# A fused linear-attention and highway kernel: a new order of all engines, eight half steps that read x from PSUM, six joint turns of k and q, and weights loaded by column halves

## The chip, the core and the metric

The kernel runs on one core of a Trainium2 chip. The metric is the device time of one execution in microseconds (us). The engines are TensorE (PE, with its weight loads as PEld), VectorE (DVE), ScalarE (ACT), GpSimd (POOL) and SyncE (SP); in this kernel SP only issues the DMA transfers.

## The reference

Two parts are computed one after the other: a linear attention with a decay per head, and a highway layer on its output.

```python
# batch 4, heads 8, sequence 768, head_dim 64; blocks of 64 positions
intra = einsum('bhic,bhjc->bhij', qb, kb) * Dmask[None]        # decay lam ** (i - j), causal
intra = einsum('bhij,bhjd->bhid', intra, vb)
inter = einsum('bhid,bhde->bhie', qb * lam_pow[None], kv_state)
out[:, :, sl] = intra + inter
kv_state = lam_block * kv_state + einsum('bhsd,bhse->bhde', kb_dec, vb)
...
x = out.transpose(0, 2, 1, 3).reshape(3072, 512)
H = maximum(x @ w_h, 0.0)
T = 1.0 / (1.0 + exp(-(x @ w_t + b_t)))
return T * H + (1.0 - T) * x                                    # float32
```

## The kernel before

**The work.** The 3072 rows are cut into twelve steps, n = 0 to 11, of 256 positions each: three steps for each batch element. A step has two half steps, b = 0 and 1, of 128 positions. For a step the kernel loads q, k and v (six transfers of 256 KB, two halves of each), casts q and k to bf16 (`CQ`, `CK`), multiplies v by powers of the decay (`CV`), and turns q and k on PE so that the head dimension lies on the partitions: `RQF` and `RKF` are eight 128x128 transposes each, into one PSUM bank each, and `EQ`/`EK` copy the result to SBUF in two halves. In step 10 `RK` and `RQ` do the same with 64-row transposes into two banks that k and q share (sixteen transposes each, L260), and `FK`/`FQ` copy them out; this is called a joint turn. Scores (`S`, L273) and the running state (`U`, L278; `KE` copies the state to SBUF) follow; `SA`/`SB` are pieces in which scores and state updates alternate. `M` masks the scores (DVE, L315), `I` (L334) and `A` (L343) give the attention output in two PSUM banks, and `D` (DVE, L349) scales it into `xT`, which is x turned.

**A half step of the highway layer.** x is turned back on PE (`TXB`, four 128x128 transposes, L362; or `TX`, sixteen 64-row transposes of a whole step, L371) and copied from PSUM to SBUF as `xs` (`XC`, ACT or DVE). `BP` puts the bias into a bank; `F.n.b.1` adds x @ w_t to it and `F.n.b.0` makes x @ w_h in another bank (four matmuls of 512 columns each, L386). Then `H` makes y = max(h, 0) - x (DVE, L399), `G` the sigmoid g (ACT, L404), `X` y = g * y (POOL or DVE, L408) and `Y` ob = y + x (POOL or DVE, L412). `ST` stores a step's 512 KB. The last half step, 11.1, is split: `P` = g * x (L415), `R` = x - P (L418), and for three column pieces `HX` = max(h, 0) * g (L422) and `YL` (L426) add the two.

**What sets the order.** No scheduler is at work. `PLAN` is a list of tokens such as `F.7.0.1.2`, `CK.9.2@ACT` or `TXB.6.1=6`, gone through from the left; each token issues its instructions on its engine, so that the order on one engine is the order of its tokens in the list. `@` names the engine, the digits behind `=` name the PSUM banks. There are seven such banks, 0 to 6, beside the bank of the running state. A token that takes a bank waits until the last reader of its former content is done. `Lq`, `Lk`, `Lv`, `W` and `ST` are transfers, all on SP's queue, at most eight of them under way at a time (L193). `W.w.g` loads half of a weight matrix (w = 1 is w_t, 0 is w_h), `WC.w.g.i` casts a quarter of one. `Z` are idle matmuls on PE at the start. The buffers in SBUF are rings: g has three, y and ob six, xs and xT three.

Of the kernel before, what the change touches and what calls it, by code (L numbers as in the profile page):

```python
# [21 lines left out]
WC.1.1.1@DVE Z.3=0 KE.1.0@ACT D.0.0@DVE Lv.2.1 WC.1.0.1@ACT WC.1.0.0@POOL M.1.0.1 U.1.1 TXB.0.0=0 BP.0.0.2@ACT=3
M.1.1.1 I.1=64 KE.1.1@ACT D.0.1@DVE F.0.0.1.2 Lk.3.1 WC.0.1.1@POOL WC.0.1.0@ACT M.1.0.0 BP.0.1.2@ACT=1 TXB.0.1=5 A.1.1
G.0.0.2 A.1.0 Lk.3.0 WC.0.0.1@DVE F.0.1.1.2 WC.0.0.0@ACT D.1.1@DVE XC.0.2.1@ACT Lq.3.1 F.0.1.0.2=2 D.1.0@DVE
XC.0.2.0@ACT Lq.3.0 G.0.1.2@S BP.1.1.2@DVE=4 TXB.1.1=5 F.0.0.0.2=0 H.0.1.2 Lk.5.1 CQ.2.2@ACT XC.1.2.1@DVE F.1.1.1.2
X.0.1.2@POOL H.0.0.2 Lv.3.1 CK.2.2@ACT BP.1.0.2@DVE=6 RQF.2=5 Lv.3.0 G.1.1.2@S Y.0.1.2@POOL TXB.1.0=1 X.0.0.2@DVE
RKF.2=2 XC.1.2.0@ACT F.1.1.0.2=0 EQ.2.1@DVE Lq.5.1 EK.2.0@ACT EK.2.1@DVE CV.2.2@POOL EQ.2.0@ACT S.2.1=14 Lk.4.1
H.1.1.2 F.1.0.1.2 M.2.0.1 Lk.5.0 CK.3.2@ACT S.2.0=25 M.2.1.1 X.1.1.2@POOL U.2.0 Lq.4.1 F.1.0.0.2=1 M.2.1.0 KE.2.0@ACT
Lq.4.0 CQ.3.2@ACT Y.0.0.2@POOL M.2.0.0 I.2=45 H.1.0.2 RKF.3=3 Lq.5.0 G.1.0.2@S A.2.1 Y.1.1.2@POOL EK.3.0@DVE
EK.3.1@ACT A.2.0 RQF.3=2 Lk.4.0 D.2.1@DVE X.1.0.2@POOL EQ.3.0@ACT D.2.0@DVE TXB.2.1=3 Lv.4.1 F.2.1.0.2=0  # L30
BP.2.1.2@ACT=1 EQ.3.1@DVE Lv.4.0 CV.3.2@POOL BP.2.0.2@DVE=6 XC.2.2.1@ACT TXB.2.0=2 F.2.1.1.2 H.2.1.2 XC.2.2.0@ACT
Lv.5.1 S.3.1=32 G.2.1.2@S S.3.0=54 Lq.6.1 Y.1.0.2@POOL M.3.0.1 U.3.0 CK.5.2@ACT F.2.0.0.2=0 Lq.6.0 M.3.1.0
X.2.1.2@POOL KE.3.0@ACT M.3.0.0 F.2.0.1.2 Lk.6.1 H.2.0.2 Lv.5.0 RKF.5=3 CQ.4.2@POOL G.2.0.2@S M.3.1.1 I.3=45 U.3.1
Lk.6.0 CK.4.2@ACT EK.5.1@DVE A.3.0 CQ.5.2@POOL A.3.1 EK.5.0@DVE RQF.4=2 D.3.0@DVE Lk.7.0 KE.3.1@ACT RKF.4=3
Y.2.1.2@POOL D.3.1@DVE BP.3.0.2@ACT=1 RQF.5=0 Lv.6.1 EQ.4.0@DVE EK.4.1@ACT TXB.3.0=6 TXB.3.1=4 EQ.5.0@DVE CV.4.2@POOL
F.3.1.0.2=5 EQ.5.1@ACT XC.3.2.0@DVE EK.4.0@DVE XC.3.2.1@ACT EQ.4.1@DVE S.5.0=60 H.3.1.2 F.3.0.1.2 CQ.6.2@ACT
X.2.0.2@POOL M.5.1.0 Lv.8.1 SA.4=3 M.5.0.0 Lv.6.0 S.4.1=42 BP.3.1.2@ACT=5 F.3.0.0.2=0 M.4.1.0 Y.2.0.2@POOL Lq.7.0
KE.4.0@ACT M.4.1.1 G.3.0.2@S F.3.1.1.2 Lk.8.1 CV.5.2@POOL H.3.0.2 CK.6.2@ACT SB.4=6 M.4.0.1 S.5.1=32 I.4=10 M.4.0.0
KE.4.1@ACT RKF.6=4 G.3.1.2@S M.5.0.1 X.3.0.2@POOL Lv.9.1 U.5.0 EK.6.0@ACT A.4.0 M.5.1.1 A.4.1 Lq.7.1 KE.5.0@ACT
RQF.6=6 X.3.1.2@POOL D.4.0@DVE EK.6.1@ACT Lq.8.0 I.5=32 EQ.6.1@DVE BP.4.0.2@ACT=5 TXB.4.0=1 Lq.9.1 D.4.1@DVE A.5.1  # L40
CV.6.2@POOL A.5.0 Lv.7.0 XC.4.2.0@DVE F.4.0.0.2=4 D.5.0@DVE Lk.7.1 D.5.1@DVE TXB.4.1=1 BP.5.0.2@ACT=0 Lk.8.0 TXB.5.0=3
F.4.0.1.2 Y.3.1.2@POOL H.4.0.2 XC.4.2.1@ACT Lv.7.1 XC.5.2.0@ACT BP.5.1.2@DVE=2 TXB.5.1=1 Lk.10.0 F.5.0.0.2=4 G.4.0.2@S
Y.3.0.2@POOL EQ.6.0@DVE Lv.8.0 XC.5.2.1@ACT BP.4.1.2@DVE=5 SA.6=3 Lq.9.0 X.4.0.2@POOL S.6.1=61 H.5.0.2 KE.6.0@ACT
F.5.0.1.2 Lk.9.1 M.6.1.0 CQ.7.2@POOL F.4.1.1.2 M.6.0.1 Lk.9.0 G.5.0.2 M.6.1.1 F.5.1.0.2=3 Y.4.0.2@POOL Lq.8.1
CK.7.2@ACT X.5.0.2@DVE F.4.1.0.2=6 H.5.1.2 G.4.1.2 CK.8.2@POOL Lk.11.0 RKF.7=1 Lk.10.1 H.4.1.2 SB.6=4 CV.7.2@POOL
EK.7.1@ACT RQF.7=0 EK.7.0@DVE KE.6.1@ACT M.6.0.0 I.6=13 RKF.8=6 EQ.7.1@ACT X.4.1.2@DVE A.6.0 EQ.7.0@ACT CV.8.2@POOL
# [450 lines left out]
```

## Time and profile before

| | |
|---|---|
| device time, median of 3 runs | 105.09 us (105.09 to 105.13) |
| device time of the profiled execution | 104.68 us |
| its span, first to last instruction | 102.9 us |
| PE busy | 92.4 us, 90% of the span |
| DVE busy | 87.2 us, 85% |
| POOL busy | 78.9 us, 77% |
| ACT busy | 76.8 us, 75% |
| transfers of SP's queue | 27.27 MB, 87.4% of 16 DMA engines |

The profiled execution's device time is 1.78 us above its span. Busy times are of single instructions laid over each other; matmuls are pipelined, so that a busy PE need not be at its peak. A line with "idle before" tells how long the engine stood still before an instruction and what ended it. "Issue" is time in which nothing that the profile shows was waited for. Line numbers are those of the kernel before; behind L232 the changed kernel's lines are higher (the masks stand at L316, H at L417, X at L426, Y at L429).

### The profile page before, as it was taken

Reading aid. Unit: us, or ns where it says so; the run is one execution under the profiler, and the core shown is the slowest. Engines: PE = TensorE matmul, PEld = TensorE weight load, DVE = VectorE, ACT = ScalarE, POOL = GpSimd, SP = SyncE. Lnnn points to the kernel's source line nnn. Section 1 sums busy time; section 2 is a strip of 40 time slices with the busy share of each in tenths; the row PEclk is TensorE's granted clock in tenths of the full one; section 3 lists DMA queues with packets and bytes.
Section 4 is the critical chain, followed back from the end, with each engine's and each line's share of the span. In section 5 each row is a group of like instructions: output and inputs, shape, how many; then the busy total and the mean of one; then the engine's idle time right before and its main releaser. Section 6 shows DMA issues by size and latency. Waiting matters only on the chain.

```text
span 102.9 us, 4082 instructions
## 1 busy us (share of the span) xinstructions
PE 92.4 (90%) x1706; PEld 57.4 (56%) x1725; DVE 87.2 (85%) x164; ACT 76.8 (75%) x132; POOL 78.9 (77%) x78
## 2 busy tenths in 40 slices
PE   5997998899898999999999989999999899999900
PEld 1443565556376668458654865846745746555400
DVE  4237989599898799999999799797997999999960
ACT  3599974999968878989587679995996675584600
POOL 6704452406999999999989995999999969689540
PEclk9999999999999999999999999999999999999997
DMA  1999999999999999999999999999991361415243
GB/s 19 272 312 317 292 369 387 354 307 287 297 322 331 329 283 293 292 294 310 331 310 300 314 310 317 323 335 395 403 380 70 128 255 37 156 48 202 111 164 138
DMA packets 33479, 27.52 MB, mean 267 GB/s; under 512 B 1460, under 2 KB 26420, under 8 KB 33461
## 3 DMA queue, kind: packets, MB, share of 16 engines
q1 hardware_dynamic: 33456, 27.27, 87.4%
q8 instruction: 13, 0.21, 0.9%
q14 instruction: 6, 0.04, 0.1%
q10 hardware_dynamic: 4, 0.00, 0.0%
HBM read 20.97 MB, written 6.29 MB: 265 GB/s over the span
## 4 chain that ended last, share of the span: by engine, by line
PE 61%; ACT 10%; SPq 9%; DMA 8%; issue 4%; DVE 3%; POOLq 1%; POOL 1%; ACTq 0%
PE bt L386 17%; PE bh L386 16%; SPq L194 9%; DMA w_f<-in_moe_w_t_dram 8%; PE bs L273 5%; PE bo L343 5%; PE bo L334 4%; PE kv L278 3%; PE bktr L244 3%; PE bx L362 3%; PE bqtr L244 3%; ACT kT L113 2%; ACT w_b L113 2%; ACT g L404 2%; ACT xs L113 1%
## 5 line engine op out<-in xcount | busy, mean ns | idle before, releaser
L315 DVE TENSOR_TENSOR m<-bs,tri 128x512 bf16<-128x512 f32 x48 | 30.8, 682 | 0.9 <-PE bs L273 0.9
L386 PEld LDWEIGHTS <-xT 128*128 128x128 bf16 x200 | 17.1, 98 | 16.9 <-issue 0.4
L408 POOL TENSOR_TENSOR y<-g,y 128x512 bf16<-128x512 f32 x17 | 19.7, 1161 | 8.1 <-DVE y L399 6.0
L412 POOL TENSOR_TENSOR ob<-y,xs 128x512 f32<-128x512 bf16 x21 | 24.1, 1159 | 0.6 <-DVE y L408 0.3
L386 PE MATMUL bh<-w_b,xT 128*128 128x512 bf16 (+2 forms) x94 | 23.8, 362 | 0.6 <-issue 0.2
L232 POOL TENSOR_TENSOR vs<-vf,pow_v 128x1024 bf16<-128x1024 f32 (+1 forms) x12 | 21.9, 1835 | 3.0 <-DMA vf<-in_v_dram 2.9
L386 PE MATMUL bt<-w_b,xT 128*128 128x512 bf16 x89 | 23.3, 380 | 0.9 <-issue 0.8
L349 DVE TENSOR_TENSOR xT<-bo,pow_o 128x512 bf16<-128x512 f32 x24 | 15.9, 683 | 0.4 <-PE bo L343 0.3
L399 DVE SCALAR_TENSOR_TENSOR y<-bh,xs 128x512 bf16<-128x512 f32 x23 | 15.6, 685 | 0.6 <-PE bh L386 0.2
L404 ACT ACTIVATE g<-bt 128x512 f32<-128x512 f32 x18 | 10.8, 598 | 4.3 <-PE bt L386 4.2
L113 ACT ACTIVATE ss<-kv 128x512 bf16<-128x512 f32 x19 | 11.3, 593 | 3.5 <-PE kv L278 3.4
L273 PE MATMUL bs<-qT,kT 64*64 64x128 bf16 x384 | 11.7, 220 | 0.5 <-ACT qT L113 0.3
L113 ACT ACTIVATE bt<-b_bc 128x512 f32<-128x512 f32 x18 | 10.7, 601 | 1.6 <-DVE xT L349 1.0
L273 PEld LDWEIGHTS <-kT 64*64 64x64 bf16 x384 | 8.1, 106 | 3.2 <-DVE kT L115 1.1
L113 ACT ACTIVATE kb<-kf 128x1024 bf16<-128x1024 f32 x9 | 9.5, 1059 | 0.2 <-DMA kf<-in_k_dram 0.2
L278 PE MATMUL kv<-vs,kb 64*64 64x64 bf16 x320 | 8.9, 195 | 0.7 <-issue 0.7
L278 PEld LDWEIGHTS <-kb 64*64 64x64 bf16 x320 | 6.9, 109 | 3.9 <-issue 2.9
L113 ACT ACTIVATE xs<-bx 128x512 bf16<-128x512 bf16 x13 | 7.5, 593 | 1.2 <-PE bx L362 0.9
L343 PE MATMUL bo<-m,vs 64*64 64x128 bf16 x384 | 8.2, 218 | 0.2 <-DVE m L315 0.2
L113 ACT ACTIVATE kT<-bktr 128x512 bf16<-128x512 bf16 x10 | 6.0, 597 | 2.8 <-DVE kT L115 1.5
L115 POOL CAST qb<-qf 128x1024 bf16<-128x1024 f32 (+1 forms) x6 | 5.8, 972 | 2.8 <-DMA qf<-in_q_dram 2.8
L115 DVE COPY kT<-bktr 128x512 bf16<-128x512 bf16 x12 | 5.0, 421 | 3.4 <-PE bktr L244 2.1
(72 smaller groups left out, 135.2 us busy)
## 6 DMA issues: line engine op xcount, KB each, us to landing
qf<-in_q_dram SPq DMA_DIRECT2D x24, 256.0 KB, 5.1
kf<-in_k_dram SPq DMA_DIRECT2D x24, 256.0 KB, 5.4
vf<-in_v_dram SPq DMA_DIRECT2D x24, 256.0 KB, 5.4
out_dram<-ob SPq DMA_DIRECT2D x11, 512.0 KB, 4.9
w_f<-in_moe_w_t_dram SPq DMA_DIRECT2D x2, 512.0 KB, 6.8
w_f<-in_moe_w_h_dram SPq DMA_DIRECT2D x2, 512.0 KB, 9.5
out_dram<-ob SPq DMA_DIRECT2D x1, 256.0 KB, 2.0
out_dram<-ob SPq DMA_DIRECT2D x2, 64.0 KB, 1.6
```

Source lines behind the costliest of these rows:

```text
L113: A.activation(dst, src, AF.Copy)
L232: ENG[eng].tensor_tensor(buf("vs", n)[:, hs], in0=buf("vf", n)[:, hs].rearrange("p h (j d) -> p h j d", j=J), in1=pow_v[:, n % NST, hs, :, ...
L273: T.matmul(get("s", n, e, hp // 2)[half(b), hp % 2, j, :], lhsT=buf("kT", n)[half(e), hp, j, half(b)], rhs=q_cols(n, half(e), hp, b), star ...
L278: T.matmul(kv[half(e), hp, half(e)], lhsT=buf("kb", n)[half(b), j, 2 * hp + e, :], rhs=buf("vs", n)[half(b), 2 * hp + e, j, :], start=firs ...
L315: V.tensor_tensor(buf("m", n, e, u), in0=get("s", n, e, u), in1=tri[:, None].to_broadcast([128, 2, J, C]), op=ALU.mult)
L343: T.matmul(get("o", n, b)[half(e), hp, :], lhsT=buf("vs", n)[half(b), 2 * hp + e, j, :], rhs=buf("m", n, e, hp // 2)[half(b), hp % 2, j, : ...
L349: V.tensor_tensor(cut(buf("xT", n)[:, :, b * C:(b + 1) * C]), in0=get("o", n, b).rearrange("e k (j p) -> e k p j", j=Q), in1=cut(pow_o[:, ...
L386: T.matmul(t, lhsT=buf("xT", n)[:, j, b * C:(b + 1) * C], rhs=w_b[w][:, j, z], start=(j == 0 and not w), stop=(j == KC - 1), skip_group_ch ...
L399: V.scalar_tensor_tensor(buf("y", n, b)[:, z], in0=get("h", n, b, p), scalar=0.0, in1=buf("xs", n)[:, b, z], op0=ALU.max, op1=ALU.subtract)
L404: A.activation(buf("g", n, b)[:, cols(p)] if to == "S" else t, t, AF.Sigmoid)
L408: ENG[eng].tensor_tensor(y, in0=buf("g", n, b)[:, cols(p)] if eng == "POOL" else get("t", n, b, p), in1=y, op=ALU.mult)
L412: ENG[eng].tensor_tensor(buf("ob", n)[:, b, z], in0=buf("y", n, b)[:, z], in1=buf("xs", n)[:, b, z], op=ALU.add)
```

## The change

All of `PLAN` is written anew. Beside the order of the tokens, four things in it differ.

- **Eight half steps (0.0, 0.1, 1.0, 4.0, 4.1, 10.0, 10.1, 11.0) read x from PSUM.** `XC`, `H`, `X` and `Y` are gone there. In their place `RP` makes r = (g - 1) * x with x read from PSUM, `HP` makes ob = max(h, 0) * g, both on DVE, and `Q` makes ob = ob - r (POOL, in 10.1 DVE).
- **Steps 6 to 11 have joint turns** (`RK`, `RQ`, `FK`, `FQ`); before, step 10 alone. Step 3 turns x by 64 rows (`TX`), as 7, 8 and 9 did before.
- **A weight transfer takes 256 columns of all rows**, in place of all columns of 256 rows. A cast takes 256 columns of two of the four row groups.
- **`SA`/`SB` are used for steps 2 to 11**; before, for 4 and for 6 to 11.

In tokens: 8 `RP`, 8 `HP` and 8 `Q` are new; `H` 23 to 15, `X` 23 to 15 (on DVE 6 to 2), `Y` 23 to 15 (on DVE 2 to 0), `XC` 24 to 16 (ACT 13 to 9, DVE 11 to 7), `BP` on DVE 6 to 3. The copies of turned q and k go from 25 to 19 on DVE and from 23 to 28 on ACT. The weight casts on POOL go from 2 to 5. `COLUMNS` is empty, so the branches that ask for it are never taken.

```diff
-Lq.0.1 Lk.0.1 Lq.1.0 Lv.0.0 Lq.0.0 Z.6=0 Lq.1.1 PW.0 Lk.0.0 Lv.0.1 Lk.1.1 CK.0.1@DVE Lk.1.0 TK.0.1=2 CQ.0.1@ACT Z.3=0
...
+Lk.0.0 Lq.0.1 Lk.0.1 Lv.0.1 Lq.0.0 Z.4=0 Lv.0.0 PW.0 Lq.1.1 Lq.1.0 CK.0.0@DVE TK.0.0=2 Lk.1.0 CQ.0.1@DVE Z.4=0 Lk.1.1
...
+COLUMNS = ()
-BUFS = dict(kf=4, qf=4, vf=4, kb=3, qb=2, vs=3, kT=2, qT=3, m=8, ss=4, xT=3, xs=3, y=6, ob=6, g=3)
+BUFS = dict(kf=4, qf=4, vf=4, kb=3, qb=2, vs=3, kT=2, qT=3, m=8, ss=4, xT=3, xs=3, y=6, ob=6, g=3, r=3)
...
     def load_w(w, g):
-        move(out=w_f[w][:, 2 * g:2 * g + 2],
-                          in_=(moe_w_h, moe_w_t)[w][256 * g:256 * g + 256].rearrange("(kc p) m -> p kc m", p=128))
+        z = slice(256 * g, 256 * g + 256)
+        move(out=w_f[w][:, :, z], in_=(moe_w_h, moe_w_t)[w].rearrange("(kc p) m -> p kc m", p=128)[:, :, z])
 
     def cast_w(w, g, i, eng):
-        copy(eng, w_b[w][:, 2 * g + i], w_f[w][:, 2 * g + i])
+        z = slice(256 * g, 256 * g + 256)
+        copy(eng, w_b[w][:, 2 * i:2 * i + 2, z], w_f[w][:, 2 * i:2 * i + 2, z])
...
+    def upper(n, b):
+        V.scalar_tensor_tensor(buf("ob", n)[:, b], in0=get("h", n, b, 2), scalar=0.0, in1=buf("g", n, b), op0=ALU.max, op1=ALU.mult)
+
+    def lower(n, b):
+        V.scalar_tensor_tensor(buf("r", n, b), in0=buf("g", n, b), scalar=1.0, in1=get("x", n, 2, b).rearrange("p k f -> p (k f)"),
+                               op0=ALU.subtract, op1=ALU.mult)
+
+    def merge(n, b, eng):
+        o = buf("ob", n)[:, b]
+        ENG[eng].tensor_tensor(o, in0=o, in1=buf("r", n, b), op=ALU.subtract)
...
+        "HP": lambda a, e, bk: upper(*a), "RP": lambda a, e, bk: lower(*a), "Q": lambda a, e, bk: merge(*a, e),
```

On SP, from the second half of step 1's k on (kf, qf, vf are the loaded k, q and v; w_f1 is w_t, w_f0 is w_h), before:

```order
L194 DMA kf1_122<-in_k_dram 128x4x128 x2
L194 DMA vf1_130<-in_v_dram 128x4x128 x2
L194 DMA w_f1_118<-in_moe_w_t_dram 128x2x512 x2
L194 DMA w_f0_117<-in_moe_w_h_dram 128x2x512 x2
L194 DMA qf2_127<-in_q_dram 128x1x512
L194 DMA kf2_123<-in_k_dram 128x4x128
```

and now:

```order
L194 DMA kf1_122<-in_k_dram 128x4x128 x2
L194 DMA vf1_130<-in_v_dram 128x4x128 x2
L194 DMA w_f1_118<-in_moe_w_t_dram 128x4x256 x2
L194 DMA kf2_123<-in_k_dram 128x4x128
L194 DMA w_f0_117<-in_moe_w_h_dram 128x4x256 x2
L194 DMA qf2_127<-in_q_dram 128x1x512 x2
```

One transfer of step 2's k now stands ahead of the two of w_h.

On POOL at the same place (vs is v with the decay, w_b the cast weights, y, g and ob as above, kb and qb the cast k and q), before:

```order
L232 TENSOR_TENSOR vs0_138<-vf0_129,pow_v_108 128x512
L232 TENSOR_TENSOR vs1_139<-vf1_130,pow_v_108 128x1024
L115 CAST w_b1_120<-w_f1_118 128x512
L115 CAST w_b0_119<-w_f0_117 128x512
L408 TENSOR_TENSOR y1_165<-g1_177,y1_165 128x512
L412 TENSOR_TENSOR ob0_170<-y1_165,xs0_161 128x512
L232 TENSOR_TENSOR vs2_140<-vf2_131,pow_v_108 128x1024
```

and now:

```order
L233 TENSOR_TENSOR vs0_138<-vf0_129,pow_v_108 128x512
L115 CAST kb1_134<-kf1_122 128x8x2x64
L233 TENSOR_TENSOR vs1_139<-vf1_130,pow_v_108 128x1024
L115 CAST w_b1_120<-w_f1_118 128x2x256 x3
L115 CAST w_b0_119<-w_f0_117 128x2x256 x2
L115 CAST qb0_136<-qf2_127 128x2x8x64
L233 TENSOR_TENSOR vs2_140<-vf2_131,pow_v_108 128x1024
```

Five of the eight weight casts, and the casts of step 1's k and step 2's q, stand on POOL now, and the first two highway instructions no longer stand between them and step 2's v.

At the end of DVE's list (bt, bh and bx are the PSUM tiles of x @ w_t, x @ w_h and turned x; ob5, y5 and y4 belong to step 11, ob4 and y3 to step 10), before:

```order
L408 TENSOR_TENSOR y3_167<-bt_2392,y3_167 128x512
L412 TENSOR_TENSOR ob4_174<-y3_167,xs1_162 128x512
L422 SCALAR_TENSOR_TENSOR bh_2451<-bh_2451,g2_178 128x128
L399 SCALAR_TENSOR_TENSOR y4_168<-bh_2477,xs2_163 128x512
L422 SCALAR_TENSOR_TENSOR bh_2484<-bh_2484,g2_178 128x128
L418 TENSOR_TENSOR ob5_175<-xs2_163,y5_169 128x512
L422 SCALAR_TENSOR_TENSOR bh_2498<-bh_2498,g2_178 128x256
L426 TENSOR_TENSOR ob5_175<-bh_2484,ob5_175 128x128
L426 TENSOR_TENSOR ob5_175<-bh_2498,ob5_175 128x256
L426 TENSOR_TENSOR ob5_175<-bh_2451,ob5_175 128x128
L412 TENSOR_TENSOR ob5_175<-y4_168,xs2_163 128x512
```

and now:

```order
L435 SCALAR_TENSOR_TENSOR r0_179<-g0_176,bx_2521 128x512
L432 SCALAR_TENSOR_TENSOR ob4_174<-bh_2532,g0_176 128x512
L440 TENSOR_TENSOR ob4_174<-ob4_174,r0_179 128x512
L443 TENSOR_TENSOR y5_169<-g2_178,xs2_163 128x512
L435 SCALAR_TENSOR_TENSOR r1_180<-g1_177,bx_2556 128x512
L432 SCALAR_TENSOR_TENSOR ob5_175<-bh_2563,g1_177 128x512
L450 SCALAR_TENSOR_TENSOR bh_2571<-bh_2571,g2_178 128x256
L454 TENSOR_TENSOR ob5_175<-bh_2571,ob5_175 128x256
L450 SCALAR_TENSOR_TENSOR bh_2577<-bh_2577,g2_178 128x128
L450 SCALAR_TENSOR_TENSOR bh_2582<-bh_2582,g2_178 128x128
L454 TENSOR_TENSOR ob5_175<-bh_2582,ob5_175 128x128
L454 TENSOR_TENSOR ob5_175<-bh_2577,ob5_175 128x128
```

DVE's last instructions are now the split half step's; half step 11.0 ends on POOL (`Q`), and its x @ w_t block stands on PE ahead of its x @ w_h block and of the three pieces of 11.1.

More of the change, by code (lines that the diff above doesn't have):

```diff
@@ L22 @@
[L22 to L46, printed above, removed]
```

120 lines of the change are left out of this document (78 added, 42 removed).

## The prediction

> **What bounds the kernel now.** First the page's head and its share of PE in the chain that ended last, then the busy time by stage: up to the first highway block (19.3 us), up to the scores of step 2 (27.2), the long middle, and what follows PE's last large block.
>
> ```profile
> span 102.9 us, 4082 instructions
> PE 61%; ACT 10%; SPq 9%; DMA 8%; issue 4%; DVE 3%; POOLq 1%; POOL 1%; ACTq 0%
> ```
>
> ```profile
> 0.00:19.30 19.30, 16.37 (x236) 8.86 (x239) 12.87 (x27) 14.22 (x26) 8.55 (x21) 1.00 0.95 287
> 19.30:27.20 7.90, 7.53 (x83) 4.30 (x84) 6.04 (x13) 7.89 (x14) 3.84 (x4) 1.00 1.12 307
> 27.20:97.30 70.10, 68.09 (x1386) 44.16 (x1403) 66.05 (x121) 54.13 (x93) 65.34 (x53) 1.00 0.87 265
> 97.30:102.90 5.60, 0.40 (x4) 0.11 (x2) 2.29 (x6) 0.60 (x1) 1.16 (x1) 0.91 0.49 171
> ```
>
> The columns behind the window's length are the busy times of PE, its weight loads, DVE, ACT and POOL, then the granted clock. In the 70.1 us of the middle PE is busy for 68.09, DVE for 66.05, POOL for 65.34: three engines within 4% of one another, at a full clock. PE comes first, and its longest waits there are small:
>
> ```profile
> PE bt L386 <- issue: 0.8, 5, 0.2
> PE bs L273 <- ACT qT L113: 0.3, 1, 0.3
> ```
>
> So the middle shrinks only if PE's work shrinks and DVE's with it. The start is another stage. There the chain runs through the weights:
>
> ```profile
> 10.31 7.78 DMA w_f<-in_moe_w_t_dram
> 18.11 0.63 ACT w_b L113
> ```
>
> The profiled execution took 104.68 us with its span of 102.9; the median of the runs shown, 105.09, is 0.41 above it. I make the sum against the profiled time and add the 0.41 at the end.
>
> **The turns of k and q (PE).** From the chain, full turns (L244, eight to a group), joint turns (L260, sixteen to a group) and the two ways to turn x:
>
> ```profile
> 64.17 0.55 PE bqtr L244 x8
> 65.17 0.45 PE bqtr L244 x8
> 63.58 0.22 PE bx L362 x4
> 71.16 0.34 PE bx L371 x16
> 77.81 0.34 PE btr L260 x16
> 78.15 0.23 PE bx L371 x16
> 78.39 0.23 PE btr L260 x16
> ```
>
> A full turn of k and one of q cost 2 x 0.45 = 0.90; joint, 0.34 + 0.23 = 0.57. Five steps change over: 5 x 0.33 = 1.65 us less. Step 3's x by 64 rows costs 0.34 in place of 2 x 0.22: 0.10 less. Sum: -1.75. The first group of sixteen costs 0.34 where it follows 128-row work and 0.23 behind other 64-row work, so entering that form costs 0.11. If all five pairs paid it once more, the saving would be 5 x 0.22 = 1.1; if none paid it, 5 x 0.44 = 2.2. I take the value between, since steps 6, 9, 10 and 11 place the joint turn next to other 64-row work, and 7 and 8 share one stretch. The Trainium skill (TensorEngine Tiling (Array Packing), Tiling Modes) states that a change of the tiling mode drains TensorE, which speaks against more changes of form. The trace agrees with 0.11 us for one; by that rule with one more drain for each pair the sum below would be 0.6 us worse. The copies that follow a turn are as many as before (four), so no engine pays for the form itself. The new alternation of scores and state updates in steps 2, 3 and 5 issues the same matmuls; I put it at nothing.
>
> **The half steps with x in PSUM.** The rows by operation and form (mean ns behind the busy time), and five neighbours on DVE that show the distance from start to start:
>
> ```profile
> L399 DVE SCALAR_TENSOR_TENSOR y<-bh,xs 128x512 bf16<-128x512 f32 x23 | 15.6, 685 | 0.6 <-PE bh L386 0.2 <-POOL ob L412 0.2 <-ACT xs L113 0.2
> L408 POOL TENSOR_TENSOR y<-g,y 128x512 bf16<-128x512 f32 x17 | 19.7, 1161 | 8.1 <-DVE y L399 6.0 <-ACT g L404 1.7 <-DVE qT L115 0.4
> L404 ACT ACTIVATE g<-bt 128x512 f32<-128x512 f32 x18 | 10.8, 598 | 4.3 <-PE bt L386 4.2
> L115 POOL CAST qb<-qf 128x1024 bf16<-128x1024 f32 x5 | 5.2, 1046 | 0.0
> ```
>
> ```profile
> 88.28 0.68 DVE L399 SCALAR_TENSOR_TENSOR y<-bh,xs 128x512 bf16<-128x512 f32 x1
> 88.88 0.68 DVE L315 TENSOR_TENSOR m<-bs,tri 128x512 bf16<-128x512 f32 x1
> 89.48 0.41 DVE L115 COPY xs<-bx 128x512 bf16<-128x512 bf16 x1
> 89.81 0.68 DVE L349 TENSOR_TENSOR xT<-bo,pow_o 128x512 bf16<-128x512 f32 x1
> ```
>
> A full DVE instruction of 128x512 costs 0.60 from start to start, a copy 0.33 to 0.34. A changed half step has two full ones (`RP`, `HP`) in place of one (`H`); the trace has neither, and both are of H's form, so 0.60 each, and 0.68 to the end of one. Counted in the list from step 2's first mask to the end, DVE had 92 full ones, 27 copies and six small ones, and now has 91, 22 and six: the extra `RP` are paid by the `X`, `Y` and `BP` that left DVE. That is -0.60 - 5 x 0.34 = -2.3 us, so DVE frees as much as PE does. On POOL `Q` stands for `X` and `Y`. From step 2's v on, its instructions of 1.16 go from 37 to 36, since DVE's own `X` and `Y` are handed to it, and its casts of 1.05 from seven to four: 1.2 + 3.1 = 4.3 us less. ACT loses four copies of x and gains five of k and q and three biases, about +1.2 us with the two weight casts gone, on an engine with 54.13 of 70.10 busy. None of this is on the path as long as PE sets the pace; I count it at nothing, and the cover is PE itself.
>
> **The start.** w_h is the last of the weights; its cast, the first block that reads it, and step 2's scores:
>
> ```profile
> 20.84 0.43 DVE L115 CAST w_b<-w_f 128x512 bf16<-128x512 f32 x1 [1.41 <-DMA w_f<-in_moe_w_h_dram]
> 21.92 1.03 PE L386 MATMUL bh<-w_b,xT 128*128 128x512 bf16 x4
> 27.23 0.42 PE L273 MATMUL bs<-qT,kT 64*64 64x128 bf16 x16 [0.35 <-ACT qT L113]
> ```
>
> Transfers by packet size: from 14 to 18 us nearly all packets are of 2 KB, from 42 to 45 us of 512 B.
>
> ```profile
> DMA packets 795, 1.55 MB, mean 387 GB/s; under 512 B 47, under 2 KB 47, under 8 KB 794
> DMA packets 1682, 0.85 MB, mean 283 GB/s; under 512 B 54, under 2 KB 1681, under 8 KB 1681
> ```
>
> Sixteen engines for 4 us over 748 packets are 85.6 ns a packet; for 3 us over 1681, 28.6 ns. The line through both has 9.6 ns for a packet of any size. A weight transfer of 256 columns has 1 KB pieces, so 2048 packets in place of 1024: 1024 x 9.6 / 16 = 0.6 us. One transfer of 256 KB that now stands ahead of w_h costs 0.26 MB / 387 GB/s = 0.7. So the last cast starts at 20.84 + 1.3 = 22.1, and with 0.63 on ACT the first h block can start at about 22.8, 0.9 later. Of this PE fills 0.44 with the two turns of step 1's x that now stand ahead of it, and the wait of 0.35 before step 2's scores can take part of the rest. I take +0.3; the ends are -0.1 (the K transfer's 0.7 alone, all of it filled) and +0.9. POOL's three casts of w_t in a row put the first t block about 0.4 later, which the same delay covers. The Trainium skill (DMA: Bandwidth & Descriptors, Specifications) gives 512 B as the smallest transfer for line rate, by which 1 KB pieces would cost nothing; the trace has 283 GB/s at 512 B against 387 at 2 KB, so here the rows decide. By the page the sum would be 0.6 lower.
>
> **The tail.** After PE's last t block:
>
> ```profile
> 97.30 0.60 ACT L404 ACTIVATE g<-bt 128x512 f32<-128x512 f32 x1 [1.03 <-PE bt L386]
> 97.98 1.16 POOL L408 TENSOR_TENSOR y<-g,y 128x512 bf16<-128x512 f32 x1 [0.87 <-ACT g L404]
> 99.17 0.69 DVE L412 TENSOR_TENSOR ob<-y,xs 128x512 f32<-128x512 bf16 x1 [0.28 <-POOL y L408]
> 65.81 0.59 SPq L194 DMA_DIRECT2D kf<-in_k_dram  x1
> out_dram<-ob SPq DMA_DIRECT2D x1, 256.0 KB, 2.0
> out_dram<-ob SPq DMA_DIRECT2D x2, 64.0 KB, 1.6
> ```
>
> From 97.30 sigmoid, gate, total and a 256 KB store follow one another: 99.86 - 97.30 = 2.6, then 3.0 to the end, 5.6 in all. Now the sigmoid comes early, half step 11.0's h block ends before the three last pieces (512 columns in all, so 0.9 us or a little less than the 1.03 of a whole block's row), and `HP` (0.7) and `Q` (1.16) follow: `Q` ends about 1.0 after PE. Behind its store two stores of 64 KB stand on SP, at 0.59 each to issue, and the last needs 1.6: 1.0 + 1.2 + 1.6 + 1.0 to the end = 4.8. That is -0.8, with ends 0 (DVE is late by one and a half instructions) and -1.6 (the small stores land with the large one).
>
> **Sum.** +0.3 - 1.75 - 0.8 = -2.3 (rounded), so 104.68 - 2.3 = 102.4 for a profiled execution and 102.8 for the median. The ends of the terms together give -3.9 to -0.2, or 101.2 to 104.9 for the forecast's own case. It holds that PE still waits as little as the rows above show.
>
> **The rivals.**
> 1. *The middle keeps its length.* The DMA engines' busy tenths in the forty slices of the span:
>
> ```profile
> DMA  1999999999999999999999999999991361415243
> ```
>
> They are full up to 77 us (slice 30), and two stores of 512 KB now stand ahead of the last two loads: 1.05 MB at 387 GB/s are 2.7 us, with the 0.6 of the weights 3.3. If loads then set the pace, PE's 1.75 is given back as waits for k and v. What is left is +0.3 - 0.8 = -0.5: 104.6. The full slices speak for it; against it speaks that none of PE's waits above ends in a transfer. Chance 0.20.
> 2. *Banks held by x (slower).* A turned x was copied out at once; now its bank stays taken until the sigmoid (0.60) and `RP` (0.60 and its place in DVE's list) are done, 1.2 later at the least, in two of seven banks at a time. In the before a stop of PE on such copies looks like this:
>
> ```profile
> 57.72 0.61 ACT kT L113
> 58.35 0.43 DVE kT L115
> 58.78 0.61 DVE m L315
> ```
>
> 1.65 us in one piece. Steps 0, 4 and 10 are the place. If each of the eight half steps stops PE for half of the 1.2, that is +4.8, and with the -2.3 the time is +2.5: 107.6. It decides from 2.3 / 8 = 0.3 us a half step on. Against it: in the new list blocks on other banks stand between the turn and the next use of its bank. Chance 0.17.
> 3. *It does not do what it says.* The joint turns hand both banks back only when k and q are both copied, and PE waits as long as it saves, while the tail is late by DVE: +0.3 - 0.1 - 0.2, no change, 105.1. Chance 0.05.
>
> The forecast has the rest, 0.58. About 0.2%, 0.2 us, is what a measurement of this kernel can tell from no change. Faster by more are the forecast and rival 1, 0.78; rival 3 is 0.05; slower is rival 2, 0.17. The range goes down to 100.8, 0.4 below the forecast's end for stops like the one of 1.65 that a new order may lose, and up to 105.3, which takes in rivals 1 and 3 and leaves rival 2 out.
>
> **What would show it.** L261 (the joint turns) with 192 matmuls at some 15 ns each in place of 32, and PE's busy time in the middle about 1.75 lower; the last w_b cast at about 22.1; DVE's last instruction on ob before the end by about 3; no row in PE's waits above 1 us. A wait of PE for `RP` (L435), many times, would be rival 2; waits for vf or kf after 60 us rival 1. Wrong altogether would be a middle as long as before with PE idle and no engine fuller than now.

## The result, and the profile after

The changed kernel takes 0.9875 of the old one's time, with an interval of 0.9845 to 0.9905: 1.3 us less than 105.32, so about 104.0. The comparison leaves out executions more than 1.5% above a kernel's fastest, which are 11 of the changed kernel's 20 (103.26 to 108.0) and none of the old one's (104.58 to 106.08); with all 20 of each the medians are 105.07 and 105.32. The forecast was 2.3 us less: 102.8 from 105.09, or 103.0 from 105.32. So something takes back about 1.0 of the 2.3 by the ratio and nearly all of it by the medians, and by amounts that differ from execution to execution.

Two executions of the changed kernel were profiled, of 107.44 us (called the first) and, in a later run, of 105.52 (the second). The page of the first:

```profile
span 105.6 us, 4229 instructions
...
DMA  1999999999999579999999934999947998550744
...
q8 instruction: 14, 0.23, 0.9%
...
PE 33%; DMA 22%; SPq 21%; ACT 10%; issue 5%; DVE 4%; POOL 2%; DVEq 0%; ACTq 0%; POOLq 0%
```

In the old kernel's chain PE had 61%, transfers and SP's issues together 17%; now 33% and 43%. The DMA engines, which were full to slice 30, have holes at slices 13 and 14 (34 to 40 us), 23 and 24 (61 to 66 us), and 29. The stages of the second execution, with the columns as before:

```profile
0.00:19.30 19.30, 15.87 (x259) 8.75 (x264) 11.38 (x24) 13.07 (x25) 10.92 (x24) 1.00 0.97 286
19.30:27.20 7.90, 7.59 (x83) 4.20 (x77) 6.42 (x11) 5.75 (x11) 3.55 (x4) 1.00 1.14 325
27.20:97.30 70.10, 65.22 (x1456) 41.60 (x1464) 63.42 (x114) 59.13 (x101) 60.32 (x48) 1.00 0.86 262
```

In the middle PE, DVE and POOL are all less busy than before (68.09, 66.05 and 65.34), ACT alone is fuller (59.13 for 54.13) and far from the bound: PE has become idle. The account of PE in four profiled executions, with the time to its last matmul split into busy and idle, and what lies behind it:

| kernel | span | PE busy | PE idle | behind PE |
|---|---|---|---|---|
| old | 102.95 | 92.39 | 5.31 | 5.25 |
| changed, first | 105.59 | 91.10 | 9.51 | 4.98 |
| changed, second | 103.57 | 89.96 | 8.62 | 4.99 |
| loads by need, weights by rows | 100.66 | 90.25 | 5.41 | 5.00 |

The last row is an experiment told below, whose half steps and joint turns are those of the changed kernel: where PE's idle time is what it was in the old kernel, the span is 2.3 us shorter, which is the prediction's sum. It is one execution, the fastest of six (102.48 to 105.71). PE's longer waits in the second execution, and the place where the first one lost most:

```profile
PE kv L279 <- POOL vs L233: 1.4, 2, 1.1
PE kv L279 <- issue: 1.0, 2, 0.5
PE bo L344 <- issue: 0.9, 1, 0.9
```

```profile
30.68 5.65 SPq L194 DMA_DIRECT2D kf<-in_k_dram  x3
...
34.91 1.04 POOL L115 CAST kb<-kf 128x1024 bf16<-128x1024 f32 x1 [1.56 <-PE kv L279]
...
36.43 0.78 SPq L194 DMA_DIRECT2D qf<-in_q_dram  x1
...
40.36 0.59 SPq L194 DMA_DIRECT2D vf<-in_v_dram  x1
...
44.76 1.06 ACT L113 ACTIVATE qb<-qf 128x1024 bf16<-128x1024 f32 x1 [2.75 <-DMA qf<-in_q_dram]
...
45.73 1.90 POOL L233 TENSOR_TENSOR vs<-vf,pow_v 128x1024 bf16<-128x1024 f32 x1 [3.61 <-DMA vf<-in_v_dram]
...
45.87 0.64 PE L245 MATMUL bqtr<-perm,qb 128*128 128x128 bf16 x5 [2.69 <-ACT qb L113]
```

The second fence is a chain over four engines. SP issues three transfers of k in 5.65 us, because the third, `Lk.8.0`, waits for the buffer that POOL's cast of step 4's k frees at 35.95. Behind it on SP stand step 5's q and v; they are asked for some 3.9 us late (three issues at 0.59 would take 1.8), ACT and POOL wait for them at 42 to 46 us, and PE waits 2.69 us for step 5's q. Then the clock falls:

```profile
42.00:45.90 3.90, 1.21 (x7) 0.36 (x6) 1.82 (x4) 1.15 (x3) 0.29 (x2) 1.00 1.09 331
45.90:49.30 3.40, 3.40 (x76) 3.20 (x78) 1.61 (x3) 1.98 (x4) 3.32 (x3) 0.51 0.95 279
```

PE busy for 1.21 of 3.9 us is followed by 3.4 us at a granted clock of 0.51. The Trainium skill (TensorE: Matmul & The Clock Gate, Part 1) says that the clock is halved after an idle window of about 3.4 us that runs freely; the trace agrees with the length, but the window was not all idle: in the last 3.41 us before it, from 42.49 on, PE was busy for 0.72.

The "issue" rows of the other fence are stops in the middle of a group of matmuls, with no releaser that the profile shows. Two theories follow. **Q**: a transfer that waits for a buffer holds up SP's queue. **I**: PE's own instructions arrive late. The `q8` row counts 14 packets of 16 KB, 0.23 MB in all; PE has 1,811 weight loads and a matmul for each (22 of these are missing from the trace), 3,622 instructions, and 256 to a packet would be 14 of them.

### The profile page after: what moved, and what is told of

The parts are those of the page before. It is cut to its first block, busy times and chain, and to the rows that moved or that the text cites. A ratio compares the mean times of both kernels' runs of the same rounds, so it can differ in the third digit from the quotient of the medians.

```text
span 105.6 us, 4229 instructions
## 1 busy us (share of the span) xinstructions
PE 91.1 (86%) x1789; PEld 56.9 (54%) x1811; DVE 84.1 (80%) x155; ACT 77.4 (73%) x134; POOL 77.5 (73%) x77
## 4 chain that ended last, share of the span: by engine, by line
PE 33%; DMA 22%; SPq 21%; ACT 10%; issue 5%; DVE 4%; POOL 2%; DVEq 0%; ACTq 0%; POOLq 0%
SPq L194 21%; PE bt L406 11%; DMA vf<-in_v_dram 11%; PE bh L406 7%; DMA qf<-in_q_dram 6%; DMA kf<-in_k_dram 5%; PE bs L274 3%; PE bo L344 3%; ACT kb L113 3%; PE bo L335 2%; ACT g L422 2%; ACT qb L113 2%; POOL vs L233 2%; DVE m L316 2%; PE bqtr L245 1%
## 5 line engine op out<-in xcount | busy, mean ns | idle before, releaser
L429 POOL TENSOR_TENSOR ob<-y,xs 128x512 f32<-128x512 bf16 x15 | 17.1, 1157 | 0.4 <-DVE y L426 0.3
L426 POOL TENSOR_TENSOR y<-g,y 128x512 bf16<-128x512 f32 x13 | 15.0, 1159 | 2.9 <-DVE y L417 1.4
L422 ACT ACTIVATE g<-bt 128x512 f32<-128x512 f32 x22 | 12.9, 594 | 3.3 <-PE bt L406 3.1
L113 ACT ACTIVATE bt<-b_bc 128x512 f32<-128x512 f32 x21 | 12.8, 609 | 2.9 <-DVE xT L350 1.7
L274 PEld LDWEIGHTS <-kT 64*64 64x64 bf16 x384 | 9.6, 109 | 3.4 <-DVE kT L115 1.4
L417 DVE SCALAR_TENSOR_TENSOR y<-bh,xs 128x512 bf16<-128x512 f32 x15 | 10.2, 685 | 0.9 <-PE bh L406 0.5
L113 ACT ACTIVATE qb<-qf 128x1024 bf16<-128x1024 f32 x7 | 7.4, 1060 | 3.2 <-DMA qf<-in_q_dram 3.2
L440 POOL TENSOR_TENSOR ob<-ob,r 128x512 f32<-128x512 f32 x7 | 8.9, 1273 | 0.2 <-DVE ob L432 0.2
L344 PEld LDWEIGHTS <-vs 64*64 64x64 bf16 x384 | 6.7, 111 | 1.3 <-issue 0.2
L245 PE MATMUL bqtr<-perm,qb 128*128 128x128 bf16 x48 | 4.0, 232 | 3.8 <-ACT qb L113 2.7
```

What stands on the lines that cost most here:

```text
L113: A.activation(dst, src, AF.Copy)
L274: T.matmul(get("s", n, e, hp // 2)[half(b), hp % 2, j, :], lhsT=buf("kT", n)[half(e), hp, j, half(b)], rhs=q_cols(n, half(e), hp, b), star ...
L344: T.matmul(get("o", n, b)[half(e), hp, :], lhsT=buf("vs", n)[half(b), 2 * hp + e, j, :], rhs=buf("m", n, e, hp // 2)[half(b), hp % 2, j, : ...
L422: A.activation(part(buf("g", n, b), n, p) if to == "S" else t, t, AF.Sigmoid)
L426: ENG[eng].tensor_tensor(y, in0=part(buf("g", n, b), n, p) if eng == "POOL" else get("t", n, b, p), in1=y, op=ALU.mult)
L429: ENG[eng].tensor_tensor(rows_of(buf("ob", n), n, b, p), in0=part(buf("y", n, b), n, p), in1=rows_of(buf("xs", n), n, b, p), op=ALU.add)
```

## The experiments

Where PLAN is a line shorter, line numbers are one or two lower than in the changed kernel.

**The changed kernel again** (the second execution above).

> The changed kernel itself, once more beside the kernel before, for a profile without the half-rate clock of the first one. Theory Q (the transfer queue): transfers on SP's queue that wait for a ring buffer hold up the loads behind them, and PE waits for the casts of those loads; then SP's list shows a gap of over 3 us between issues near 31 to 36 us, and the time is 103.3 to 105.5. Theory B (banks held by x): PE's waits are on DVE's r = (g - 1) * x, and the queue's gaps cost nothing.

It took 0.9981 of the old kernel (0.994 to 1.0022), which is no change that can be told, so the 0.9875 of the result is not repeated; the next three kernels, run on the same chip, are set against this one. At 39.09 and 80.62 us PE stops without a releaser for 0.47 and 0.90; the wait of 2.69 for step 5's q is gone, and one of 1.13 for step 5's v stands at 46.72. SP's three issues of k, from 31.33 on, take 3.94 us here, 5.65 in the first execution. The same program loses at different places.

**One transfer later.**

```diff
-... M.3.0.1 Lk.8.0 RKF.4=4 ...
-... TXB.4.1=6 Lk.8.1 ...
+... M.3.0.1 RKF.4=4 ...
+... TXB.4.1=6 Lk.8.0 Lk.8.1 ...
```

> The changed kernel with one transfer moved: the first half of step 8's k (Lk.8.0), which in the profile of after waited from about 31 to 36 us with four loads of step 5 behind it, stands just ahead of the other half (Lk.8.1). Theory Q: the gap near 31 to 36 us and the wait of step 5's casts go, 1 to 2.5 us less than the changed kernel. Theory B: no difference over 0.3 us.

No ratio came of it: six executions from 102.81 to 107.53, median 106.2, where the changed kernel beside it had 105.4. So the 1 to 2.5 us that theory Q foretold did not show. The block at 31 us is gone, but the profiled execution (107.46) shows others:

```profile
38.52 8.30 SPq L193 DMA_DIRECT2D qf<-in_q_dram  x2
...
40.84 0.26 PE L278 MATMUL kv<-vs,kb 64*64 64x64 bf16 x2 [2.23 <-issue]
...
56.91 2.52 SPq L193 DMA_DIRECT2D vf<-in_v_dram  x3
61.79 0.55 SPq L193 DMA_DIRECT2D qf<-in_q_dram  x1
...
70.46 2.00 ACT L112 ACTIVATE kb<-kf 128x1024 bf16<-128x1024 f32 x2 [2.42 <-DMA kf<-in_k_dram]
72.37 0.58 ACT L421 ACTIVATE g<-bt 128x512 f32<-128x512 f32 x1
73.00 0.39 PE L260 MATMUL btr<-id,kb 64*128 64x64 bf16 x15 [1.10 <-ACT g L421]
```

PE's stop without a releaser of 2.23 us stands at the place of the 0.47 above, and the 3.4 us from 40.8 on have a granted clock of 0.51. It reaches SP too: the second of two issues of q (38.52) waits for the buffer that the cast of step 5's q, late behind PE, frees at 46.26, and from 44.2 to 47.6 the DMA engines are busy for 0.02. The other is Q's alone: SP stands before step 11's q until 61.79, because its buffer is freed by the cast of step 7's q at 61.77; step 9's k is issued behind it, and ACT waits for that k until 70.46; behind the casts in ACT's list stands a sigmoid, and the next joint turn needs that sigmoid's bank.

**All loads in the order of need.** Six loads move behind those that are needed sooner, and the last ones ahead of the first stores; the other engines' lists are as in the changed kernel. SP's alone:

```diff
-... Lk.5.0 Lk.8.0 Lq.5.1 ... Lk.6.1 Lq.8.1 Lq.9.0 Lv.6.0 ... Lv.7.0 Lv.9.1 Lk.10.0 Lq.7.1 Lk.8.1 ... Lv.8.1 Lq.11.1 Lk.10.1 ... Lq.10.1 ST.0 Lq.10.0 Lk.11.1 Lq.11.0 ST.5 Lk.11.0 Lv.11.1 ST.3 ...
+... Lk.5.0 Lq.5.1 ... Lk.6.1 Lv.6.0 Lk.7.0 Lq.8.1 Lq.8.0 ... Lq.7.1 Lk.8.0 Lk.8.1 Lv.9.1 ... Lk.10.0 Lk.10.1 Lq.9.0 Lq.9.1 ... Lq.10.1 Lq.10.0 Lk.11.1 Lq.11.1 Lq.11.0 Lk.11.0 Lv.11.1 ST.0 ST.5 ST.3 ...
```

> The changed kernel with nine transfers moved, so that none that needs the buffer of a step four before stands ahead of loads needed sooner, and the last five loads stand ahead of the first two stores. Order on all other engines as in the changed kernel. Theory Q: 2 to 3.5 us less than the changed kernel, about 101.5 to 102.8, and less scatter. Theory B: within 0.3 us of the changed kernel.

0.9824 (0.977 to 0.9877), where the changed kernel had 0.9981 (0.994 to 1.0022) on the same chip: Q's blocks were worth about 1.6%, or 1.6 us, a little under the 2 to 3.5 foretold. The DMA engines are full to slice 27, and after 20 us PE waits for no cast longer than 0.4 us. The stops without a releaser have stayed:

```profile
DMA  1899999999998999999999999999698460551743
...
PE bt L405 <- issue: 2.2, 6, 1.4
PE kv L278 <- issue: 1.0, 1, 1.0
```

**Weights by rows** (`load_w` and `cast_w` as in the old kernel).

> The changed kernel with the weights loaded and cast by rows as before (2 KB pieces in place of 1 KB), all else as changed. By the packet sum of the prediction the last weight lands 0.6 us sooner, and the time is 0.2 to 0.6 us less if the start is on the path. Theory Q: the start is not what binds, less than 0.3 us of difference.

0.9893 (0.9843 to 0.9942). Step 2's scores begin at 26.62 us, in the changed kernel's second execution at 26.92: by these two the 1 KB pieces cost 0.3. One execution is little to go by: with 1 KB pieces and the same lists up to there, four profiles have 26.77 to 27.50. The rest of the 0.9 us between the two ratios, whose intervals touch, has no cause shown.

**Both together, and pieces of PE's list shifted.** The last two edits in one kernel; then the same with 88 (the diff) and with 40 more instructions (14 of 146 columns) at the start of PE's list, where it spins.

```diff
         t = bank(("spin", idle[0]), bk[0], [128, 512])
+        r, c = (26, 80) if idle[0] <= 2 else (r, 512)
         for _ in range(r):
-            T.matmul(t, lhsT=id128, rhs=blank, start=True, stop=True)
+            T.matmul(t[:, :c], lhsT=id128, rhs=blank[:, :c], start=True, stop=True)
```

> The changed kernel with both edits at once: the loads on SP in the order of need, and the weights by rows (2 KB pieces). All other lists are as in the changed kernel. Theory Q (transfers that wait for a ring buffer hold up the ones behind them on SP) and the price of the weights' 1 KB pieces are separate, so the gains add: .9824 for the one and .9893 for the other against the old kernel, where the changed kernel had .9875; about .980 is expected here, some 103.0 us. Theory I (TensorE's own instructions arrive late) says that PE's stops in the middle of a group stay, since PE's list is the same: at 38 to 41, 74 to 76 and 79 to 81 us, 1 to 2.5 us in all, and that they are what still scatters from run to run. The rival, that all of it was Q, expects no stop without a releaser above 0.2 us in the middle and a span below 101.

> As the kernel with loads in the order of need and weights by rows, but the first two spins of four matmuls of 512 columns are 26 each of 80 columns: 88 more instructions on PE (44 matmuls, 44 weight loads) in a time in which PE has nothing else to do, at the same number of columns (4160 for 4096). Theory I: PE's instructions come in pieces of 256, and PE stops where it uses up one piece in less than the 5 us or so in which the next comes. With 88 more in front, the pieces begin 88 instructions earlier in the work; by the trace of the kernel with weights by rows the shortest pieces now take 4.0 us (76.7 to 80.7) and 4.7 (60.9 to 65.6), and those that took 3.7 (from 34.1) and 4.35 (from 73.1) are gone. So the stops at 38 to 41 and at 74 to 80 vanish; one of up to 1.2 us may stand at 81. Faster than the kernel without the 88 by 0.5 to 1.5 us. Rival: where the pieces end does not matter, and the time is the same or 0.1 longer.

> The same with 14 matmuls of 146 columns in each of the first two spins: 40 more instructions on PE at the same number of columns (4088). Theory I: now four pieces are short, 3.7 us (33.8 to 37.5), 4.0 (57.1 to 61.1), 4.7 (61.0 to 65.7) and 3.8 (77.2 to 81.0), so stops of about 0.5 to 1.5 us without a releaser stand at about 38, 62 and 82, places at which no kernel stopped so far; slower than the one without them by 0.5 to 2 us, and than the one with 88 by 1.5 to 3. Rival: no difference among the three.

Both edits: six executions from 102.48 to 105.71 (median 104.57, where about 103.0 was foretold), and no ratio. With 88 more: 0.9765 (0.9715 to 0.9815). With 40 more: 0.9842 (0.9798 to 0.9885). In the profiled execution with both edits alone (102.48) the only stop without a releaser above 0.3 us after 20 us is 0.51 at 38.97. Those with 88 more (first) and with 40 more:

```profile
67.48 0.24 PE L342 MATMUL bo<-m,vs 64*64 64x128 bf16 x1 [1.44 <-issue]
...
73.40 0.41 PE L272 MATMUL bs<-qT,kT 64*64 64x128 bf16 x13 [0.40 <-issue]
```

```profile
17.32 0.25 PE L342 MATMUL bo<-m,vs 64*64 64x128 bf16 x4 [0.60 <-issue]
...
62.95 0.30 PE L272 MATMUL bs<-qT,kT 64*64 64x128 bf16 x5 [1.21 <-issue]
```

The stops have moved to work that had not stopped in any profile. In PE's list they stand where they always do. Over all 14 profiles there are 20 stops of over 0.3 us without a releaser after 15 us, and each begins within 8 instructions of number 189 + 256 n, a place that PE passes some 180 times in them. The trace of single packets shows why:

| kernel | PE enters a piece of 256 | next 16 KB packet | PE goes on | stop |
|---|---|---|---|---|
| old | 12.61 | 15.71 to 16.80 | 18.28 | 0.70 |
| one transfer later | 34.73 | 38.16 to 39.20 | 40.84 | 2.23 |
| 88 more | 61.15 | 64.81 to 66.02 | 67.48 | 1.44 |
| 40 more | 57.56 | 60.50 to 61.38 | 62.95 | 1.21 |
| full turns (below) | 37.52 | 42.14 to 43.24 | 44.53 | 1.19 |

The packet for a piece starts up to 4.6 us after PE has entered the one before it, takes about 1.1, and PE goes on 1.3 to 1.6 after its end. A piece that PE uses up in less leaves it without instructions; the five of the table were used up in 3.9 to 5.8 us. Theory I is shown for the places. Which of them stop, and for how long, was not foretold: with 40 more the kernel was to be slower than without, and of the three places named (38, 62 and 82) only 62.95 was hit; with 88 more nothing stopped at 81, and the stops at 67.48 and 73.40 were not named. When the packet starts differs from one execution to the next.

**The old kernel with step 8's k early.**

```diff
-... Lk.7.1 Lk.8.0 Lv.7.1 ...
+... Lv.5.1 Lk.8.0 Lq.6.1 ...
```

> The old kernel with one transfer moved: the first half of step 8's k stands right behind the second half of step 5's v on SP, 13 places earlier, with the last q of step 6, a half of step 6's k and the last half of step 5's v behind it. Its buffer is free when ACT has cast step 4's k, at 39.03 us in the old kernel's trace, and SP reached this place at 34.64. Theory Q: SP stands still for about 4.4 us, the DMA engines run dry for part of it, step 5's v and step 6's q and k come later by up to 4 us, and PE, which had no wait on a transfer, gets waits of 0.5 to 3 us between 40 and 55 us: slower by 0.5 to 3 us (ratio 1.005 to 1.03). Rival: the list has slack there, the DMA engines catch up, and the time is the same within 0.3 us.

1.0243 (1.0197 to 1.0289), but not by the way expected. The transfer stands ahead of step 4's cast in the program, so SP does not wait for the cast (it waits 3.1 us for the buffer's older load to land); the cast waits for the transfer, and step 4 computes with half of step 8's k:

```profile
41.44 1.06 ACT L112 ACTIVATE kb<-kf 128x1024 bf16<-128x1024 f32 x1 [2.47 <-DMA kf<-in_k_dram]
...
42.55 0.62 PE L243 MATMUL bktr<-id,kb 128*128 128x128 bf16 x8 [2.17 <-ACT kb L112]
```

It shows only that the old order, too, loses 2.5 us where one cast is late (41.44, in the old kernel's profile 37.97), and it says nothing on a block of SP by a cast. After this stop of 2.17 us the clock stays at 1.00.

**Fewer transfers under way** (on the kernel with 88 more).

```diff
-UNDER_WAY = 8
+UNDER_WAY = 5
```

> As the kernel with loads in the order of need, weights by rows and 88 more instructions, but at most five transfers of SP's queue under way at a time in place of eight. In the traces so far the packet of 16 KB that brings PE's next 256 instructions starts 0.9 us after PE goes over into a new piece where the DMA engines have little to do (after 85 us), and 2 to 4 us after it where they are full. Theory I with a queue behind it (the packet waits for data packets that are under way): fewer of them make it start earlier, by up to 3/8 of the wait, about 1 us; stops without a releaser then stay under 0.5 us, and the times lie closer together, 101.8 to 103. Rival: the packet waits its turn among the data whatever their number, the start stays at 2 to 4 us, and the time is the same, or some tenths longer since loads are issued later.

Theory and rival both came true in part. No stop above 0.3 us without a releaser is left; between 20 and 75 us the 16 KB packet starts 0.3 to 2.0 us after PE enters a piece, where it had been 1.0 to 3.7. That it waits behind data that is under way is not shown by this: in the changed kernel's first execution, with eight under way, it starts 0.1 to 3.5 us after, on average 1.5 as here. The kernel is slower, 1.0102 (1.0014 to 1.0191). Its profiled execution (108.79) had a granted clock of 0.95 for most of the span, where the other profiles had 1.00 outside their stretches at half clock, so neither its time nor its lack of stops is a measure of the edit alone. It shows late loads and stores:

```profile
73.30 12.68 SPq L193 DMA_DIRECT2D out_dram<-ob  x6
...
79.86 1.16 POOL L427 TENSOR_TENSOR ob<-y,xs 128x512 f32<-128x512 bf16 x1 [4.88 <-DMA out_dram<-ob]
...
85.03 0.39 PE L370 MATMUL bx<-id,xT 64*128 64x64 bf16 x15 [1.94 <-ACT g L420]
```

POOL waits 4.88 us for an output buffer whose store comes late, the gate and the sigmoid's buffer behind it, and PE 1.94 for the sigmoid's bank; SP takes 12.68 us to issue six stores.

**The changed kernel with 88 more and nothing else.**

> The changed kernel with nothing but the 88 more instructions on PE in front (the first two spins as 26 matmuls of 80 columns each); SP's list and the weights are as in the changed kernel. Theory I alone: stops at 38 to 41 and at 74 to 81 us go, faster than the changed kernel by 0.5 to 1 us (ratio to the old kernel about .980 where the changed kernel had .9875 and .998). Theory Q alone: SP stands still at 31 to 35 us as before, and the waits of PE for vs and qb stay (1 to 3 us in all), so that it stays 1 to 2 us behind the kernel that also has the order of need and weights by rows (.9765). Both are expected here: between the two.

0.9878 (0.979 to 0.9965). After 20 us no stop without a releaser above 0.3 is left, and Q's are (ACT waits for step 9's k again, and the second line follows from the first as at 73.00 above):

```profile
68.19 2.00 ACT L113 ACTIVATE kb<-kf 128x1024 bf16<-128x1024 f32 x2 [3.04 <-DMA kf<-in_k_dram]
...
70.73 0.39 PE L261 MATMUL btr<-id,kb 64*128 64x64 bf16 x15 [1.23 <-ACT g L422]
```

The interval covers the changed kernel's 0.9875, so the gain by shift alone is not shown.

**Full turns of k and q** (on the kernel with 88 more; the same for steps 7 to 11).

```diff
-... RK.6=15 ... RQ.6 ... FK.6.0@ACT ... FK.6.1@ACT FQ.6.0@DVE ... FQ.6.1@ACT ...
+... RKF.6=1 ... RQF.6=5 ... EK.6.0@ACT ... EK.6.1@ACT EQ.6.0@DVE ... EQ.6.1@ACT ...
```

> As the kernel with loads in the order of need, weights by rows and 88 more instructions, but k and q of steps 6 to 11 turned in full (eight matmuls of 128 rows each for k and for q) in place of jointly by 64 rows (16 and 16); the copies out of PSUM stay where they are. PE has 192 fewer instructions. By the prediction's term, six pairs at 0.33 us: PE's busy time grows by 2.0, and the time by 1.5 to 2. Theory I takes some of it back: 192 fewer instructions are three quarters of a piece, so from step 6 on there are fewer short pieces; by it the time grows by 0.5 to 1.5. Rival: the copies of a full turn can start after half of the matmuls, and the engines behind them gain what PE loses; then the time is the same within 0.5.

0.9846 (0.9805 to 0.9888) against 0.9765 (0.9715 to 0.9815): 0.85 us slower, inside the 0.5 to 1.5 of theory I, though the two were measured on different chips and the intervals touch. The turns of steps 7 and 8 with what stands around them, full and then joint (the kernel with 88 more):

```profile
59.32 0.39 PE L361 MATMUL bx<-id,xT 128*128 128x128 bf16 x4
59.55 0.61 PE L243 MATMUL bktr<-id,kb 128*128 128x128 bf16 x8
...
60.89 0.61 PE L243 MATMUL bqtr<-perm,qb 128*128 128x128 bf16 x8
61.33 1.03 PE L404 MATMUL bt<-w_b,xT 128*128 128x512 bf16 x4
```

```profile
58.60 0.39 PE L361 MATMUL bx<-id,xT 128*128 128x128 bf16 x4
58.93 0.41 PE L259 MATMUL btr<-id,kb 64*128 64x64 bf16 x16
...
59.40 0.40 PE L259 MATMUL btr<-id,kb 64*128 64x64 bf16 x16
59.64 0.40 PE L259 MATMUL btr<-perm,qb 64*128 64x64 bf16 x16
59.97 1.04 PE L404 MATMUL bt<-w_b,xT 128*128 128x512 bf16 x3
```

A full turn takes 0.45 from start to start, a joint one 0.23 to 0.24 behind another. But the turn of x ahead of a joint one takes 0.33 where it took 0.23, and the last joint turn ahead of 128-row work 0.33: each of these two changes of form costs 0.10. So the two pairs take 2.01 in full and 1.37 jointly, 0.32 for a pair; over all six places it is 2.3 us. From step 2's scores on, PE's busy time is 68.03 against 66.27, 1.76 more, and 0.85 is seen in the time. PE's idle time is 5.44 in the profiled execution, 7.07 in that with joint turns, the slowest of its six; its stops without a releaser (1.19 against 1.44 and 0.40) are 0.65 of that difference, and the rest has no cause shown. Its twelve executions also lie closer together, 102.75 to 104.63, than the six with joint turns, 101.78 to 104.51.

**The old kernel with 88 more.**

> The old kernel with nothing but 88 more instructions on PE in front: its first two spins (six and three matmuls of 512 columns) are 35 of 88 and 18 of 85 columns, 4610 columns in place of 4608. In its trace no piece of 256 instructions is used up in less than 4.6 us after the first 18 us; with 88 more in front two are, 3.8 us (from 44.9) and 3.8 (from 70.3). Theory I: stops of PE without a releaser of 0.3 to 1.5 us at about 48.7 and 74, places at which the old kernel does not stop; slower by 0.5 to 2 us (ratio 1.005 to 1.02), with times that scatter more. Rival: the old order is not sensitive to it, ratio 1.00 within 0.003.

1.0066 (1.0026 to 1.0105), inside theory I's 1.005 to 1.02, with a stop at 75.50 us that the old kernel does not have; none stands at 48.7, the other place named:

```profile
75.50 0.25 PE L273 MATMUL bs<-qT,kT 64*64 64x128 bf16 x4 [0.32 <-issue]
```

A stop of 0.32 in this one execution doesn't account for all of the 0.7 us. Step 2's scores begin at 27.42, in the old kernel's profile at 27.23, so a part may also lie in the start.

## Why the prediction was right, and where it was wrong

By the ratio of the result the direction and the range hold, and the size, 102.8 against about 104.0, is nearer to rival 1's 104.6. That the direction holds is not firm: over all 20 executions the medians differ by 0.25, and the second measurement of the same kernel (0.9981, 0.994 to 1.0022) is no change.

- *Turns of k and q, -1.75.* Right in size: a pair at steps 7 and 8 saves 0.32 where I charged 0.33. From step 2's scores on, PE's busy time is 68.49 in the old kernel, 66.78 in the second execution and 66.26 with both edits, 1.7 to 2.2 less (other small changes are in it). The drain for each change of form of the Trainium skill (TensorEngine Tiling (Array Packing), Tiling Modes) shows as 0.10 at each of these places (0.33 in place of 0.23), on the way into 64-row work and on the way out.
- *The start, +0.3.* It came out at -0.3 in the second execution. The last w_b cast and the first h block are close to the 22.1 and 22.8 named, but step 2's scores are earlier than 27.23:

```profile
21.79 0.43 DVE L115 CAST w_b<-w_f 128x512 bf16<-128x512 f32 x1 [0.23 <-DMA w_f<-in_moe_w_h_dram]
...
22.47 2.76 PE L406 MATMUL bh<-w_b,xT 128*128 128x512 bf16 x12
...
26.92 0.84 PE L274 MATMUL bs<-qT,kT 64*64 64x128 bf16 x24
```

  By one pair of executions the smaller pieces cost 0.3, where I had 0.6 and the page of the Trainium skill (DMA: Bandwidth & Descriptors, Specifications) nothing; the step that failed is that PE could not fill the delay. How far it failed is open: the same start gave 26.77 to 27.50 in four profiles of the new order, and the old order 27.23 and 28.12 in two.
- *The tail, -0.8.* It is -0.25: 5.25 us behind PE's last matmul before, 4.97 to 5.01 in all profiles of the new order with eight transfers under way. I took 5.6 from the end of the last t block, though PE had pieces of an h block to do until 97.70, and set against it 4.8 from PE's end: two starting points in one difference. From the new one, `Q` ends 1.3 after PE, not 1.0 (98.65 + 1.27 against 98.58).

```profile
98.65 1.27 POOL L440 TENSOR_TENSOR ob<-ob,r 128x512 f32<-128x512 f32 x1 [0.18 <-DVE ob L432]
```

- *DVE, POOL and ACT at nothing.* Right as a price: DVE's busy time is 87.25 before and 84.14 in the second execution, POOL's 78.88 and 77.20. (The copies of turned q and k on DVE go from 25 to 20, not to 19.) What failed is the sentence below the sum, "It holds that PE still waits as little as the rows above show": PE's idle time went from 5.31 to 9.51 and 8.62. The sign against it, a row above 1 us in PE's waits, is there. This is the step that cost most of the gain.
- *Rival 1* said that loads would set the pace because the DMA engines are full. Its sign was seen (ACT waits for kf at 65 to 70 us), but not its cause: the engines run dry, since SP stands before a transfer whose buffer is not free (61.79 above). With the loads in order and the same bytes 1.6% come back.
- *Rival 2* is refuted: the only wait of PE for `RP` (L435) in any profile is one of 0.23, with five under way. Banks are waited for where a sigmoid is late (73.00, 70.73, 85.03), and that comes from a transfer. *Rival 3* named 105.1, which is near the second measurement, but by another way: no profile has PE waiting for the copies of a joint turn to hand a bank back.

So of the 2.3 us a part that differs from execution to execution is taken back, by SP's blocks and by stops for instructions. That the sum of 2.3 is met where PE's idle time stays (the last row of the table) is in part luck: the turns came out as charged, but the tail gave 0.5 less and the start 0.6 more. That the executions which were not profiled differ by the same two causes is likely from the profiles that were, but not shown.

## What to carry to other kernels

A gain that is counted on the engine that sets the pace holds only as long as everything that feeds it stays ahead: after a reordering, go down the transfer queue and ask of each transfer when its buffer comes free, and what stands behind it. Put the loads in the order of need before judging the rest; here that alone was worth about 1.6%, and joint turns in place of full ones about 0.8%. Of an engine with many small instructions, count how fast it uses them up, and where the time scatters look for stops without a releaser.

## What was not expected of the hardware

PE's instructions are fetched in packets of 16 KB, 256 at a time, which the page counts on the core's 16 DMA engines beside the data, and a stop of up to 2.23 us follows when 256 of them are used up before the next packet is in; in five such places they were used up in 3.9 to 5.8 us. The Trainium skill (Runtime: NRT & Kernel Launch, Instruction fetch mechanics) states the 16 KiB blocks, with which the 14 packets agree, and that their fetch is mostly hidden; here it is hidden at most of some 180 places, but 20 stops of 0.32 to 2.23 us show that it is not always. 88 instructions more at the start made the old kernel slower by 0.7% (1.0066, 1.0026 to 1.0105), of which one stop of 0.32 us was seen. The fastest kernel of all, 0.9765 (0.9715 to 0.9815), is the changed one with its loads in the order of need, its weights by rows and its instructions shifted by 88. Whether it owes part of that to where its pieces happen to end is not shown: shifted by 40 it has 0.9842 (0.9798 to 0.9885), and the two intervals overlap.
